# Key weights transposed on their way in, by two DMA queues, in a linear-attention and SiLU block

## The chip, the cores and the metric

The kernel runs on one core of a Trainium2 chip. A core has TensorE (PE, which does the matmuls and loads their weights), VectorE (DVE), ScalarE (ACT), GpSimd (POOL), SyncE (SP), and 16 DMA engines that carry what SP and ACT issue. The metric is the device time of one execution in microseconds (us); the median over runs is compared.

## The reference, cut to what matters

```python
h  = x + attention(layernorm(x))          # x: 2048 rows of 640, bf16
h2 = h + silu(layernorm(h) @ w1) @ w2     # w1: 640 x 1728, w2: 1728 x 640

# attention: 32 heads of width 20
q, k, v = split(xn @ wqkv)
pq, pk  = q @ w_phi[h], k @ w_phi[h]                     # per head, 20 x 20
phi_q   = [softmax(pq), softmax(-pq)]                    # over the 20 features
phi_k   = [softmax(pk), softmax(-pk)]
kv      = sum over rows of phi_k^T v;   z = sum over rows of phi_k
o       = (phi_q @ kv) / (phi_q . z);   result = o @ wo
```

## The kernel before

The 2048 rows are 16 tiles of 128 rows (`t` = 0 to 15); the 640 columns are 5 chunks of 128 (`c`). Each small operation is a Python function `op_xx`, and the string `ORDER` (lines 25 to 62) is a list of words such as `kp.3` (call `op_kp(3)`). Within one engine, and within each DMA queue, instructions run in the order of the words that concern it; the block `tc.manual_schedule` (line 678) fixes these orders, and the framework adds the semaphore waits that the data needs. A letter at a word's end names an engine or a queue: `.s` issues a DMA on SP, `.a` on ACT (or copies on ACT), `.v` works on DVE, `.p` on POOL. An instruction that waits holds back all that comes after it on its engine, DMA issues included.

Stages, and the words that the text uses:

- Head. `lx` loads tiles of x, `lp` loads `w_phi`, `lk` loads the key weights (tile `wk`), `lv` the value weights. `ph` (L189) spreads `w_phi` into a block form, `phb`, which uses the mask from `mk`. Key weights and `w_phi` are folded into one matrix, `Wfk`: `wt.c` transposes chunk `c` of `wk` on PE (five 128x128 transposes, L296), `wc.c` copies the result out of PSUM into `wTk`, `fk.c` multiplies with `phb` (six matmuls, L311), `fc.c` copies the result into `Wfk`. The query weights are folded in the same way (`gk`, `gc`, also L311), but they are read transposed: `lq.c` (L234) is a transposing DMA from DRAM, issued on SP into the tile `wTq`, which is the tile `wk` again, so that `lq.c` waits for `wt`.
- Layernorm of x: `st.t` (DVE statistics, L254 and L255), `rs` (POOL), `xn.t` (normalise, on DVE L271 or ACT L276), and a transpose of the tile, either on PE with a copy (`xt`, `xc`) or by a transposing DMA on SP (`xd`, L289).
- Keys and values, per tile: `kp` and `vp` (ten matmuls of 320 columns each, L339), `ke` (two exponentials, ACT, L361), `kr` (sums and reciprocals, DVE, L369 and L372), `ka` (product, POOL, L377; `kb` does half a tile on DVE), `vc` (copy of the values), `cc` (twenty small matmuls which add the tile to `kv`, L399). `km` (L409) masks the finished `kv`.
- Queries, in groups of four tiles: `qp.g.i` (matmuls of 512 columns, L419) and `qe` (exponentials, L429).
- From `dp.0` on (L453), which needs the finished `kv`: attention output per tile, normalisation, transposing DMA `td` (L508), projection `op` (L515), second layernorm, transposing DMA `hd` (L574), then `up` (L589), SiLU `ua` (L611), `yp` (L635) and the stores. This stage's orders are new too, its operations are the same. `ta` is a small exponential on ACT (L244), which makes ACT load the table of Exp at that point.

The warm-up: six matmuls of 512 columns on a zero tile ahead of the first word, with `ident` as the stationary operand, and `wm.256` or `wm.512` among the words (L248). Each `wm` among the words takes a PSUM buffer of its own. The pool `mm` has four such buffers, and every `wt`, `fk`, `gk`, `xt`, `kp`, `vp` and `wm` takes the next in turn, which waits until the user of that buffer four steps before has been copied out.

Of the kernel before, what the change touches and what calls it, by code (L numbers as in the profile page):

```python
# [34 lines left out]
xd.15 gk.0 kr.5 vp.9 ka.1.p gc.0.a xn.7.a kp.9 ke.8 xd.7 xn.12.v kr.0 ka.5.p kp.6 vc.9.a xd.11
xn.10.a kp.15 ke.6 xd.12 ka.0.p xd.13 cc.2 kr.6 cc.1 ke.15 cc.5 xd.10 vp.15 ke.9 kr.3 ka.6.p kp.11
vc.15.a xn.14.a kr.4 gk.1 vp.7 gc.1.a ka.3.p xd.14 ke.11 vp.11 lo.s l2.8.13.s vc.7.a kr.11 l1.0.s
ka.4.p vp.6 vc.11.a kp.13 kr.15 vc.6.a ka.11.p kp.12 kr.9 cc.4 ka.15.h cc.3 ke.12 cc.6 kr.8 cc.0
ka.9.p cc.11 ke.13 kp.14 kr.12 gk.3 ke.14 kp.10 ka.8.p gc.3.v kp.7 ke.10 kr.14 ka.12.p qp.1.2 ke.7
vp.14 kr.13 qe.1.2 qp.0.1 vc.14.a kr.7 ka.13.p vp.12 qe.0.1 ka.14.p vp.13 vc.12.v vp.10 vc.13.v  # L40
ka.7.p kr.10 qp.0.0 vc.10.a kb.15 ka.10.p qp.0.2 cc.13 qe.0.2 cc.15 cc.14 qe.0.0 cc.9 cc.7 cc.12
cc.10 cc.8 qp.2.2 km.1 close km.0 dp.0 qe.2.2 qp.1.1 dw.0.v dp.2 qe.1.1 dr.0 qp.1.0 dw.2.v do.0.0.p
do.0.1.p dp.3 qe.1.0 dr.2 qp.3.0 dw.3.v do.2.0.p dp.6 qe.3.0 dr.3 qp.2.0 dw.6.v do.3.0.p do.3.1.p
do.2.1.p td.3 dp.4 qe.2.0 dr.6 qp.3.1 dw.4.v td.0 do.6.0.p td.2 dp.1 qe.3.1 dr.4 qp.2.1 dw.1.v
do.4.0.p do.4.1.p do.6.1.p td.4 dp.5 qe.2.1 dr.1 op.0 dw.5.v do.1.0.p do.1.1.p qp.3.2 td.1 oa.0 dp.8
l1.2.s qe.3.2 dr.5 op.3 l2.4.8.s dw.8.v do.5.1.p sq.0 sa.0 op.1 sr.0 td.6 oa.3 do.5.0.p op.2 dr.8
td.5 oa.1 do.8.0.p dp.9 hn.0 do.8.1.p sq.1 op.4 dw.9.v sa.1 td.8 sr.1 op.6 hd.0 hn.1 oa.2 hd.1 op.5
oa.4 sa.2 sq.2 op.8 oa.6 sq.4 oa.5 sq.6 dp.7 sa.5 up.0.1 dw.7.v sa.6 sr.6 sr.2 up.0.2 oa.8 ua.0.1
dr.9 sa.8 sq.8 hn.6 do.9.0.v sr.8 do.9.1.v up.0.3 ua.0.2 dr.7 td.9 do.7.1.p dp.10 sq.5 up.0.0
do.7.0.p dw.10.v td.7 hd.6 op.9 hn.2 ua.0.0 hn.8 ua.0.3 hd.8 dp.12 sq.3 oa.9 op.7 sa.9 sq.9 yp.0.1  # L50
sr.9 oa.7 dw.12.v sq.7 sa.7 yp.0.0 sr.7 sa.4 hn.7 sa.3 yh.0.0 dr.10 hd.7 dp.11 hn.9 sr.4 yp.1.0
dw.11.v hd.9 do.10.1.p sr.3 yp.1.1 hd.2 do.10.0.v yo.0 dr.12 dp.14 hn.3 do.12.0.p up.2.2 dr.11
dw.14.v sr.5 do.11.0.p up.2.5 do.11.1.p ua.2.2 hn.4 dr.14 hd.4 hn.5 yo.1 do.12.1.v up.2.6 hd.3
ua.2.5 td.10 dp.15 up.2.4 dw.15.v td.12 td.11 op.10 do.14.1.v hd.5 dr.15 up.2.3 oa.10 sa.10 op.11
ua.2.3 sq.10 up.1.4 oa.11 ua.2.6 do.15.1.v sa.11 ta do.15.0.p up.1.1 do.14.0.p td.14 sq.11 up.2.1
td.15 ua.1.4 ua.1.1 up.1.3 ua.2.1 ua.2.4 up.1.6 ua.1.3 dp.13 ua.1.6 op.15 op.12 oa.15 dw.13.v sa.15
op.14 sr.10 up.1.5 sr.11 dr.13 hn.11 oa.14 up.2.0 do.13.1.v sa.14 sq.14 oa.12 ua.1.5 sa.12 do.13.0.p
up.1.2 ua.2.0 td.13 so.1 up.1.0 ua.1.2 sq.15 sr.15 op.13 ua.1.0 hn.15 sq.12 yp.5.1 oa.13 sa.13 sq.13
sr.14 yp.5.0 sr.12 yh.1.1 sr.13 yh.2.0 yo.5 yp.8.0 hn.10 hn.13 hd.13 yp.3.0 yp.6.0 hn.14 yp.8.1
yp.4.0 yo.8 so.8 hd.10 yp.6.1 so.0 yp.3.1 hn.12 hd.12 yp.4.1 yo.3 yo.6 so.3 hd.11 yp.2.0 hd.15  # L60
yp.9.0 hd.14 so.5 yh.1.0 yh.2.1 yp.9.1 yp.7.1 yo.9 yo.4 yp.7.0 so.4 so.9 so.6 up.4.0 yo.7 so.7
up.3.1 yp.2.1 ua.3.1 up.4.1 yo.2 ua.4.0 up.4.3 up.3.0 up.3.5 ua.3.0 ua.4.3 ua.4.1 up.3.3 up.3.4
ua.3.3 ua.3.5 up.4.2 up.3.6 ua.4.2 ua.3.4 up.3.2 ua.3.6 yp.15.0 ua.3.2 yp.10.0 yp.14.1 yh.3.0 yh.4.0
yp.12.1 yp.14.0 yp.12.0 yo.14 yp.15.1 yo.12 so.12 yp.11.1 yo.15 yp.11.0 so.15 so.14 so.2 yp.10.1
yh.3.1 yo.10 yq.13.0 yo.11 so.11 so.10 yq.13.1 yz.13.0 yz.13.1 sz.13.0.a sz.13.1.s
"""

@with_exitstack
def kernel(
# [41 lines left out]
    def mm2():  # L111
        return mm.tile([P, 2, 512], F32, name="mm2")
# [11 lines left out]
    wTk = first.tile([P, C, D], BF16, name="wTk")  # L124
# [3 lines left out]
    ident = persist.tile([P, P], BF16, name="ident")  # L128
    make_identity(nc, ident[:])
    warm = first.tile([P, 512], BF16, name="warm")  # L130
# [87 lines left out]
    def dma(q, out_, in_):  # L218
        (nc.sync if q == "s" else nc.scalar).dma_start(out_, in_)
# [13 lines left out]
    def op_lq(c):  # L233
        nc.sync.dma_start_transpose(wTq[:, :, c * P : (c + 1) * P], A_wqkv[c * P : (c + 1) * P, 0:D])  # L234

    def op_lo(q="s"):
        dma(q, wo[:], A_wo.rearrange("(c p) n -> p c n", p=P))

# [6 lines left out]

    def op_wm(n=512, ps=None):
        ps = mm2() if ps is None else ps
        nc.tensor.matmul(ps[:, 0, 0:n], ident[:], warm[:, 0:n], start=True, stop=True)  # L248
        return ps

    def op_st(t):
# [425 lines left out]
    ops = {k[3:]: f for k, f in locals().items() if k.startswith("op_")}  # L677
    with tc.manual_schedule(engines={PE, SP, POOL, DVE, ACT}):
        ps = None
        for i in range(6):  # L680
            ps = op_wm(512, ps)
        for word in ORDER.split():
            name, *args = word.split(".")
            ops[name](*[int(a) if a.isdigit() else a for a in args])
# [27 lines left out]
```

## Time and profile before

| | us |
|---|---|
| median of three runs | 243.97 (243.68 to 245.48) |
| the profiled execution's own time | 245.96 |
| span of the profiled execution, first to last instruction | 244.2 |
| PE busy | 234.6 |
| first warm-up matmul | 1.52 |
| first projection (`vp.1`) | 12.52 |
| first matmul of `dp.0` | 74.23 |
| last instruction on PE ends | 240.46 |

Times in the views count from the span's start. A timeline row gives start, length, engine, line of the kernel, the operation with what it writes and reads, and how many instructions were merged in the row. SPq and ACTq are the issuing side of the two DMA queues; an issue is not the transfer, whose time to landing stands in the DMA view. Busy PE is not PE at its peak, since matmuls overlap: the pitch of a row (its length over its count) tells more than the mean of one.

### The profile page before, as it was taken

How to read it: one execution, taken by the hardware profiler on the slowest of the kernel's cores; microseconds unless marked ns; L12 is line 12 of the kernel's file. 1: busy time of each engine (PE TensorE's matmuls, PEld its weight loads, DVE VectorE, ACT ScalarE, POOL GpSimd, SP SyncE). 2: the span in 40 equal slices, each digit the busy share in tenths (PEclk: the TensorE clock that was granted, in tenths of full speed). 3: DMA queues.
4: the chain of work that ended last, by engine and by line, in shares of the span. 5: the costliest groups of instructions: out<-in, count | busy, mean ns of one | idle time of the engine just before them, and what ended most of it. 6: DMA issues, size and time to landing. Idle time of an engine off the chain costs nothing.

```text
span 244.2 us, 5190 instructions
## 1 busy us (share of the span) xinstructions
PE 234.6 (96%) x2146; PEld 151.9 (62%) x2160; DVE 131.6 (54%) x252; ACT 108.1 (44%) x158; POOL 90.7 (37%) x172
## 2 busy tenths in 40 slices
PE   6999999998999999899899999999999999999995
PEld 3777677775674456577564545646776765556762
DVE  3599996899627999986597620722222310000223
ACT  3678988857444675266403098074000022450000
POOL 4244897997941446543473030325000000000000
PEclk9999999999999999999999999999999999999999
DMA  6899858580000046933442511020136300000022
GB/s 201 290 261 240 179 88 129 129 301 0 3 3 3 0 82 143 253 26 66 44 82 56 108 29 27 1 54 4 27 82 136 107 30 0 0 3 0 10 100 81
DMA packets 42968, 20.60 MB, mean 84 GB/s; under 512 B 34368, under 2 KB 42560, under 8 KB 42944
## 3 DMA queue, kind: packets, MB, share of 16 engines
q1 hardware_dynamic: 42368, 19.65, 34.9%
q10 hardware_dynamic: 576, 0.62, 0.7%
q8 instruction: 17, 0.28, 0.5%
q14 instruction: 7, 0.06, 0.1%
HBM read 9.61 MB, written 2.62 MB: 50 GB/s over the span
## 4 chain that ended last, share of the span: by engine, by line
PE 76%; DMA 9%; DVE 7%; ACT 3%; issue 2%; POOL 1%; ACTq 0%; SPq 0%; POOLq 0%
PE mm L635 23%; PE mm L589 21%; PE mm L419 9%; PE mm L339 8%; PE mm L515 6%; DVE Sk L369 3%; PE mm L453 2%; DMA X<-in_A_x_dram 2%; DMA wk<-in_A_wqkv_dram 2%; DMA ot<-o 2%; DMA XnT<-xn 2%; DMA HnT<-hn 2%; PE mm L399 2%; ACT Ek L361 1%; PE mm L650 1%
## 5 line engine op out<-in xcount | busy, mean ns | idle before, releaser
L589 PE MATMUL mm<-HnT,w 128*128 128x512 bf16 (+1 forms) x318 | 57.8, 336 | 0.6 <-DMA HnT<-hn 0.2
L635 PE MATMUL mm<-w,shT 128*128 128x320 bf16 (+2 forms) x415 | 57.8, 299 | 0.2 <-issue 0.2
L611 ACT ACTIVATE shT<-mm 128x1024 bf16<-128x1024 f32 (+2 forms) x29 | 27.0, 963 | 65.7 <-PE mm L589 64.2
L635 PEld LDWEIGHTS <-shT 128*128 128x128 bf16 x416 | 39.8, 98 | 17.5 <-issue 1.1
L589 PEld LDWEIGHTS <-w 128*128 128x128 bf16 x325 | 31.3, 98 | 23.7 <-issue 0.5
L658 DVE TENSOR_TENSOR ob<-mm,X 128x640 bf16<-128x640 f32 x15 | 12.2, 822 | 53.7 <-PE mm L635 44.7
L339 PEld LDWEIGHTS <-XnT 128*128 128x128 bf16 x320 | 30.8, 98 | 13.4 <-issue 0.8
L377 POOL TENSOR_TENSOR Ek<-Ek,Sk 128x1280 bf16<-128x1280 bf16 (+1 forms) x16 | 36.6, 2321 | 3.6 <-DVE Sk L372 2.3
L429 ACT ACTIVATE EqT<-mm 128x1024 bf16<-128x1024 f32 (+1 forms) x24 | 19.8, 881 | 12.8 <-PE mm L419 12.8
L515 PE MATMUL mm<-wo,ot 128*128 128x320 bf16 x160 | 23.4, 299 | 1.8 <-DMA ot<-o 1.8
L339 PE MATMUL mm<-Wfk,XnT 128*128 128x320 bf16 x160 | 23.5, 299 | 1.2 <-DVE Wfq L159 0.6
L369 DVE TENSOR_REDUCE Sk<-Ek 128x64 f32<-128x1280 bf16 x16 | 23.2, 1448 | 2.4 <-ACT Ek L361 2.4
L488 POOL TENSOR_TENSOR o<-u,rd 128x320 bf16<-128x320 f32 x25 | 18.0, 736 | 16.8 <-DVE rd L482 7.5
L419 PE MATMUL mm<-XnT,Wfq 128*128 128x512 bf16 x94 | 23.1, 380 | 0.4
L339 PE MATMUL mm<-wv,XnT 128*128 128x320 bf16 x160 | 23.2, 299 | 0.0
L361 ACT ACTIVATE Ek<-mm 128x640 bf16<-128x640 f32 x32 | 20.5, 708 | 5.7 <-PE mm L399 3.2
L524 DVE SCALAR_TENSOR_TENSOR X<-mm,X 128x640 bf16<-128x640 f32 x16 | 12.9, 818 | 17.4 <-PE mm L515 17.3
L515 PEld LDWEIGHTS <-ot 128*128 128x128 bf16 x160 | 15.2, 98 | 8.6 <-DMA ot<-o 2.3
L532 ACT ACTIVATE sq<-X 128x640 bf16<-128x640 bf16 x16 | 11.7, 734 | 15.5 <-DVE X L524 15.5
L537 POOL TENSOR_SCALAR HM<-HST 128x1 f32<-128x1 f32 x16 | 3.4, 213 | 34.3 <-DVE X L524 34.3
L419 PEld LDWEIGHTS <-Wfq 128*128 128x128 bf16 x100 | 9.2, 97 | 10.2 <-issue 0.3
L254 DVE BATCH_NORM_STATS2 stats<-X 128x6 f32<-128x320 bf16 x32 | 13.7, 469 | 2.9 <-DMA X<-in_A_x_dram 2.9
(73 smaller groups left out, 209.9 us busy)
## 6 DMA issues: line engine op xcount, KB each, us to landing
out_dram<-ob SPq DMA_DIRECT2D x15, 160.0 KB, 1.9
w<-in_B_w_dram SPq DMA_DIRECT2D x3, 720.0 KB, 5.0
X<-in_A_x_dram SPq DMA_DIRECT2D x3, 640.0 KB, 5.5
w<-in_B_w_dram SPq DMA_DIRECT2D x2, 640.0 KB, 6.3
wo<-in_A_wo_dram SPq DMA_DIRECT2D x1, 800.0 KB, 5.0
w<-in_B_w_dram SPq DMA_DIRECT2D x1, 800.0 KB, 6.6
X<-in_A_x_dram SPq DMA_DIRECT2D x4, 160.0 KB, 4.4
wv<-in_A_wqkv_dram SPq DMA_DIRECT2D x2, 320.0 KB, 4.8
```

What stands on the lines that cost most here:

```text
L254: nc.vector.bn_stats(stats[:, k, :], X[:, t, k * 320 : (k + 1) * 320])
L339: nc.tensor.matmul(ps[:, half, 0:320], tok(XnT[t // GT], t)[:, c, :], W[:, c, half * 320 : (half + 1) * 320], start=(c == 0), stop=(c == C ...
L361: nc.scalar.activation(Ek[:, s, :].rearrange("p (a n) -> p a n", a=2), tl["kp", t][:, :, 0:320], AF.Exp, scale=1.0 - 2.0 * s,)
L369: nc.vector.tensor_reduce(Sk[:], tl["ek", t][:].rearrange("p s (h f) -> p (s h) f", f=DH), axis=AX.X, op=ALU.add,)
L377: eng.tensor_tensor(Ek3, Ek3, tl["sk", t][:, lo:hi].unsqueeze(2).to_broadcast([P, hi - lo, DH]), op=ALU.mult,)
L419: nc.tensor.matmul(ps[:, k, :], Wfq[:, c, r * P : (r + 1) * P], XnT[g][:, c, :], start=(c == 0), stop=(c == C - 1),)
L429: nc.scalar.activation(E[:, s, rs[0] : rs[-1] + 1, :], tl["qp", g, i][:, 0 : len(rs), :], AF.Exp, scale=1.0 - 2.0 * s,)
L488: (nc.vector if eng == "v" else nc.gpsimd).tensor_tensor(tl["o", t][:, a * 320 : (a + 1) * 320].rearrange("p (h f) -> p h f", f=DH), tl["u ...
L515: nc.tensor.matmul(ps[:, half, 0:320], tl["ot", t][:, c, :], wo[:, c, half * 320 : (half + 1) * 320], start=(c == 0), stop=(c == C - 1),)
L589: nc.tensor.matmul(ps[:, i * W : (i + 1) * W], w1[:, c, fc * P : (fc + 1) * P], HnT[g][:, c, 0:W], start=(c == 0), stop=(c == C - 1), skip ...
L611: nc.scalar.activation(sh[:, a:b], tl["up", g, k][:, 0 : b - a], AF.Silu)
L635: nc.tensor.matmul(ps, shT[g][:, fc * W + i * P : fc * W + (i + 1) * P], w2[:, fc, a:b], start=first and fc == 0, stop=last and fc == FC - ...
```

## The change

`wTk` is no longer made on PE. A new word, `lt.c`, reads chunk `c` of the key weights transposed from DRAM straight into `wTk`, on SP (`.s`) or ACT (`.a`): three on SP, two on ACT. The words `lk`, `wt` and `wc` are gone, and `lq` no longer shares its tile with a loaded `wk`. The warm-up takes a part of the zero tile as the stationary operand instead of `ident`, has eight matmuls instead of six, and ten `wm` among the words instead of six (five of them of 512 columns). `ORDER` is another list for all engines: in the head tiles 3, 2 and 0 come first instead of 1 and 0, all five folds of the key weights stand before the first projection, the loads of x and of the value weights are spread over both queues, and 30 query matmuls stand ahead of `dp.0` instead of 35. `ta` moves from among the SiLU calls to a place among the last exponentials of the keys. The diff, with the list cut to the part up to the second half of the key stage:

```diff
 ORDER = """
-lk.4.5.a lx.1.2.s lk.2.3.a lp.s lk.0.1.a lk.3.4.s mk lx.0.1.s lk.1.2.s lv.4.5.s lv.0.2.s st.1
-lv.2.4.s wt.2 lx.2.3.s wt.4 wc.2.a ph rs.1 lx.3.4.s wm.256 wm.256 wt.0 lx.4.8.s wc.4.a xn.1.v wc.0.a
-wm.256 wm.256 fk.4 st.0 wt.3 fc.4.a fk.2 wt.1 wc.3.a xt.1 rs.0 wc.1.v lq.4 fc.2.a wm.256 fk.3 fk.1
-xn.0.v fc.3.a fk.0 xc.1.v lx.8.12.s fc.0.a lx.12.16.s wm.256 xt.0 vp.1 lq.3 st.2 xc.0.a fc.1.a st.3
-vp.0 lq.2 st.4 rs.3 l2.0.4.s kp.0 vc.0.a lh.s rs.2 xn.3.v vc.1.a st.5 gk.4 ke.0 xt.3 xn.2.v kp.1
-rs.4.2 st.8 xc.3.a xn.4.v xt.2 ke.1 st.9 vp.3 xd.4 xn.5.v gc.4.a st.11 kp.3 xd.5 xc.2.a st.10 kp.2
-l1.1.s ke.3 st.13 rs.8.4 vp.2 ke.2 st.6 rm.8 rm.9 st.14 mo gk.2 vc.3.a kp.5 xn.8.a st.15 rm.10
-gc.2.a mc xd.8 kp.4 st.12 vc.2.a xn.9.a st.7 lq.1 vp.4 ke.5 rs.12.4 kr.2 lq.0 vp.5 ke.4 rm.11 rm.14
-xd.9 rs.6.2 vc.4.a xn.13.v vp.8 xn.15.v xn.11.a rm.7 xn.6.v ka.2.p kr.1 xd.6 vc.5.a kp.8 vc.8.a
-xd.15 gk.0 kr.5 vp.9 ka.1.p gc.0.a xn.7.a kp.9 ke.8 xd.7 xn.12.v kr.0 ka.5.p kp.6 vc.9.a xd.11
-xn.10.a kp.15 ke.6 xd.12 ka.0.p xd.13 cc.2 kr.6 cc.1 ke.15 cc.5 xd.10 vp.15 ke.9 kr.3 ka.6.p kp.11
-vc.15.a xn.14.a kr.4 gk.1 vp.7 gc.1.a ka.3.p xd.14 ke.11 vp.11 lo.s l2.8.13.s vc.7.a kr.11 l1.0.s
...
+lp.a lx.3.4.s lx.2.3.a lt.3.s lt.4.a mk lt.1.s mc lx.0.1.a lx.1.2.a lt.2.s lt.0.a ph st.3 lq.0
+lx.4.8.a wm.512 wm.512 fk.4 lv.0.2.a st.2 wm.512 wm.256 fk.1 rs.3 fc.4.a lv.2.4.s fk.3 fc.1.a
+lx.8.12.s xn.3.v wm.512 wm.256 fk.2 rs.2 lq.3 fc.3.a st.0 wm.256 xt.3 fk.0 fc.2.a xn.2.v fc.0.a lq.1
+rs.0 wm.512 wm.256 gk.0 xc.3.v xt.2 lv.4.5.a wm.256 kp.3 xn.0.v xc.2.a lq.4 gc.0.a st.4 xt.0
+lx.12.16.a kp.2 lq.2 xc.0.a st.5 st.1 kp.0 rs.4.2 ke.2 rs.1 xn.4.v vp.0 ke.3 st.6 xd.4 mo xn.1.v
+ke.0 vp.3 st.7 lh.s vc.0.a st.11 rs.6.2 gk.2 gk.4 gc.2.a kp.4 xn.5.v rm.6 st.10 gc.4.a xd.5 vc.3.a
+gk.3 xn.7.v gk.1 st.8 xd.7 vp.4 gc.1.a gc.3.a st.9 l1.1.s xt.1 vc.4.a vp.2 l1.2.s st.14 rs.8.4
+xc.1.a ke.4 st.13 kp.5 rm.11 rm.10 st.15 vc.2.a kp.1 xn.6.a st.12 xn.11.a kp.7 xn.9.v rs.12.4 ke.1
+kr.4 xd.9 vp.7 ke.5 rm.8 rm.12 lo.s rm.13 kr.0 ka.4.p xn.10.a qp.0.1 vc.7.a xd.10 ke.7 kr.2 ka.0.p
+vp.9 xd.11 xn.13.a qe.0.1 kr.3 vp.5 xd.13 ka.2.p xd.6 kp.9 vc.9.a kr.5 xn.12.a l2.4.8.s vp.1 ke.9
+ka.3.p xd.12 xn.15.v kp.11 kr.1 vc.5.a l2.8.13.s ka.5.p cc.2 cc.4 xn.14.v ke.11 cc.0 kr.9 xd.14 cc.3
+kp.13 vc.1.a ka.1.p l1.0.s xn.8.a kr.11 kp.10 ke.13 xd.8 vp.6 ka.9.p ke.10 xd.15 vp.10 l2.0.4.s
+kr.10 kp.6 vc.10.a vc.6.a kr.13 ka.10.p kp.14 ke.6 kp.8 kr.7 ka.11.h cc.5 ka.13.p cc.9 kr.6 ke.14
+cc.1 cc.10 vp.11 kr.14 ka.6.p vp.8 vc.11.a ke.8 qp.0.2 ka.14.p vc.8.a kr.8 vp.12 kp.12 vc.12.a kb.11
...
 """
         nc.sync.dma_start_transpose(wTq[:, :, c * P : (c + 1) * P], A_wqkv[c * P : (c + 1) * P, 0:D])
 
+    def op_lt(c, q="s"):
+        (nc.sync if q == "s" else nc.scalar).dma_start_transpose(
+            wTk[:, :, c * P : (c + 1) * P], A_wqkv[c * P : (c + 1) * P, D : 2 * D],
+        )
+
     def op_lo(q="s"):
         dma(q, wo[:], A_wo.rearrange("(c p) n -> p c n", p=P))
 
@@ -245,7 +250,7 @@
 
     def op_wm(n=512, ps=None):
         ps = mm2() if ps is None else ps
-        nc.tensor.matmul(ps[:, 0, 0:n], ident[:], warm[:, 0:n], start=True, stop=True)
+        nc.tensor.matmul(ps[:, 0, 0:n], warm[:, 0:P], warm[:, 0:n], start=True, stop=True)
         return ps
 
     def op_st(t):
@@ -677,7 +682,7 @@
     ops = {k[3:]: f for k, f in locals().items() if k.startswith("op_")}
     with tc.manual_schedule(engines={PE, SP, POOL, DVE, ACT}):
         ps = None
-        for i in range(6):
+        for i in range(8):
             ps = op_wm(512, ps)
         for word in ORDER.split():
             name, *args = word.split(".")
```

## The prediction

> **What bounds the kernel now.** I read the page's busy parts first, then the timeline of the head, then who keeps PE waiting, then the DMA views.
>
> ```profile
> PE 234.6 (96%) x2146; PEld 151.9 (62%) x2160; DVE 131.6 (54%) x252; ACT 108.1 (44%) x158; POOL 90.7 (37%) x172
> PE   6999999998999999899899999999999999999995
> ```
>
> PE bounds nearly the whole span. A change can win only in the head (first two digits), in PE's few waits, and in the tail.
>
> Timeline, PE (start, length, line; a bracket holds the idle time before):
>
> ```profile
> 1.52 2.74 PE L248 MATMUL mm<-warm,ident 128*128 128x512 bf16 x6 [1.52 <-POOL ident masks.py:199]
> 8.02 0.76 PE L311 MATMUL mm<-phb,wTk 128*128 128x140 bf16 x6
> 12.52 2.88 PE L339 MATMUL mm<-wv,XnT 128*128 128x320 bf16 x20
> 24.26 0.48 PE L311 MATMUL mm<-phb,wk 128*128 128x140 bf16 x6
> 74.23 0.57 PE L453 MATMUL mm<-KVBD,EqT 64*128 64x88 bf16 x20
> ```
>
> Dense projections start at 12.52 and run into `dp.0` at 74.23. The same fold costs 0.76 us at 8.02 and 0.48 at 24.26: PE is slow until about 10.7, though the granted clock reads 1.00 throughout.
>
> Who kept PE waiting (us in total, times, longest):
>
> ```profile
> PE mm L515 <- DMA ot<-o: 1.8, 2, 1.2
> PE mm L248 <- POOL ident masks.py:199: 1.5, 1, 1.5
> PE mm L296 <- DMA wk<-in_A_wqkv_dram: 0.7, 2, 0.4
> PE mm L339 <- DVE Wfq L159: 0.6, 1, 0.6
> PE mm L339 <- DMA XnT<-xn: 0.5, 1, 0.5
> PE mm L589 <- DMA HnT<-hn: 0.2, 1, 0.2
> PE mm L635 <- issue: 0.2, 1, 0.2
> ```
>
> All but the second and third lie behind 12.52: 3.3 us is the most that new orders can win there.
>
> Timeline, ACT's and SP's queues, and the ScalarE table load:
>
> ```profile
> 0.79 1.46 ACTq L219 DMA_DIRECT2D wk<-in_A_wqkv_dram  x3
> 0.79 0.40 SPq L219 DMA_DIRECT2D X<-in_A_x_dram  x1
> 2.28 1.28 ACT L161 ACT_TABLE_LOAD   x1 [2.28 <-issue]
> 10.47 1.29 SPq L234 DMA_TRANSPOSE wk<-in_A_wqkv_dram  x1
> ```
>
> An issue holds its queue 0.46 us for a plain load, 1.3 for a transpose. The table load stands behind all of ACT's first issues.
>
> DMA view of the stretch around 10.5, then the queues of the whole run:
>
> ```profile
> wk<-in_A_wqkv_dram SPq DMA_TRANSPOSE x1, 2.9
> ```
> ```profile
> q1 hardware_dynamic: 42368, 19.65, 34.9%
> q10 hardware_dynamic: 576, 0.62, 0.7%
> ```
>
> From issue to landing a 160 KB transpose takes 2.9 us on a quiet queue (median of the five 4.2, longest 7.4). ACT's queue, q10, carries 576 packets of about 1 KB, plain loads and one store: before never transposes on two queues.
>
> **The change part by part.** The sum goes against the profiled execution: span 244.2, its run 245.96. The median of the three runs is 243.97; I carry the change of span over to it.
>
> Removed: five `wk` loads, 25 PE transposes (`wt`, about 0.53 us per five) and five copies (`wc`, 0.5 to 0.7 each), all ahead of 12.52. Nothing later needs them.
>
> Added: five transposed loads, in the order `lt.3.s lt.4.a lt.1.s lt.2.s lt.0.a lq.0` over both queues. The framework sets this program's waits; the orders do not. How it treats transposes from two queues no row shows. From below it costs nothing (both queues run abreast; a gain over that has no source). From above, a transpose of one queue is held until those of the other have landed: four hand-overs of a landing each, 2.9 to 7.4 us. I take the upper kind: I read the framework, which orders by semaphores whatever it counts as sharing a path, as letting the transposes of only one queue run at a time. And I take 2.9 for each, because the first X load at 0.79, also on quiet queues, lands after 3.1.
>
> The Trainium skill, "DMA: Bandwidth & Descriptors", section "DMA Transpose (X-bar)", speaks for this: two streams of transposes in flight corrupt each other, so the later must wait for the earlier's full completion. By that rule the hand-over is needed; without it the sum would be that of rival 1 below. No run here shows it.
>
> The walk: SP issues X at 0.79 and `lt.3` at 1.25, landing 4.15. ACT, held there, issues `lt.4`, landing 7.05. SP, held, issues `lt.1` at 7.15 and `lt.2` at 8.5, landing 11.4. ACT issues `lt.0` at 11.45, landing 14.35. Behind the waits stand, on SP, `lq.0 lv.2.4 lx.8.12` and the other `lq` (from 14.4); on ACT, `lx.0.1 lx.1.2` (5.5) and, after `lt.0` (12.75), `lx.4.8 lv.0.2` (2 x 0.46), the table load (1.28), and so `fc.4` at 15.0. That is the costly part: ACT's five weight copies stand in its program behind the last transpose.
>
> From 15.0 PE and ACT alternate, because four PSUM buffers are shared by folds and warm-ups: `fk.3` waits for `fc.4`'s buffer, `fk.2` for `fc.1`'s, `gk.0` for `fc.0`'s. At warm prices (fold 0.35 to 0.48, copy 0.70, transposes 0.28) the first projection `kp.3` starts at 19.4; at the cold ones of 8.02 to 10.9 (fold 0.76, transposes 0.58) at 20.7. PE sits nearly idle from 9 to 15, so most is cold: 20.3.
>
> One sentence stands apart: the Trainium skill, "TensorE: Matmul & The Clock Gate", Part 1, has the clock fall to half after an idle window of about 3.4 us, which agrees with the 0.76 against 0.48; warm all along it would be 19.4.
>
> Warm-up: eight 512-column matmuls at 0.43 (2.74 over six, less one latency) and two more, from 1.25 instead of 1.52, as they need only DVE's memset. They end by 5.6; nothing waits for PE before 7.05. Fillers between folds lie beside ACT's copies. Both cost nothing; were the copies faster, each filler would cost 0.11 to 0.43 us.
>
> `ta` moves into the Exp stage: two table loads of 1.28 go where ACT waits 64.2 us for PE in all. Nothing.
>
> From `kp.3` to `dp.0`: 32 projections x 1.36 = 43.5; four Wq folds x 0.35 = 1.4; two tile transposes, 0.5; sixteen `cc` x 0.43 = 6.9; 30 query matmuls x 0.216 = 6.5 (before did 35 there). Sum 58.9, so 79.2. From `dp.0` to PE's end before: 240.46 - 74.23 = 166.2, less its waits of 2.2, plus the five query matmuls 1.1: 165.1. Tail unchanged: 244.2 - 240.46 = 3.7. Waits under the new order: between 0 and the present 3.3, middle 1.7.
>
> Is PE still the last at `dp.0`? DVE stands still at `xc.3` until 19.1; then 13 statistics x 1.0, six `xn` x 0.4 and the first Sk, 2.0, give 36.5. POOL's sixteen products (36.6 busy, 3.6 waiting in before) end at 76.7, one `cc` and one mask later 77.8: 1.4 ahead of PE. Late X tiles are what comes next: `lx.4.8` now issues at 12.75, before by 7.4.
>
> Sum: 20.3 + 58.9 + 165.1 + 1.7 + 3.7 = 249.7, against 244.2: +5.5. On the median about 249.5; I say 249.8 for the extra hops of the four hand-overs.
>
> **The rivals.**
>
> 1. No hand-over: queues abreast (ends on the other side). ACT issues `lt.0` at 3.97, its last load by 6.2, table load to 7.5, and the same chain at warm prices puts `kp.3` at 11.9. Sum 11.9 + 58.9 + 165.1 + 1.7 + 3.7 = 241.3, -2.9: 241.1 on the median, 239.4 with no waits, 242.7 with 3.3. For it: no row shows a wait between queues, and the issue order alternates. Against it: all 49 transposes of before are issued by SP (q1) while q10 is nearly empty, so no row shows two queues transposing at once either, and my reading of the framework. It decides when one hand-over costs under about 1 us.
>
> 2. POOL or DVE sets `dp.0`. If `lx.4.8` or `lx.8.12` land as late as the 7.4 us that loads near 12.9 took, DVE's statistics start 1 to 2.5 us later and POOL passes PE: `dp.0` near 81.5, time 251.8. For it: the 1.4 us of slack. Against: the needed tiles come first in DVE's order.
>
> 3. The hand-overs come cheaper: landing 2.6 as the on-chip transposes, all warm, all waits closed: 249.5 - 1.2 - 0.9 - 1.6 = 245.8.
>
> **How the numbers follow.** Forecast 0.65; rival 1 0.14; rival 2 0.15; rival 3 0.06. Time 249.8. From the unknowns: low is rival 3, 246.0; high is rival 2 with landings of 3.5 instead of 2.9 (+2.2), 254.0. Rival 1 and the edges are left out, under 0.2. One per cent of 243.97, about what a measurement here can tell, puts the bounds at 241.5 and 246.4. Rival 1 splits 0.08 faster, 0.06 same; of rival 3 0.02 is same; the rest is slower: 0.84.
>
> **What would show it.** Right: the `lt` issues as rows on both queues with starts near 1.3, 4.2, 7.2, 8.5 and 11.5, ACT's queue held; ACT's table load near 14; first L344 matmul near 20; `dp.0` near 80; PE waits on copies in the head. Wrong: all five issues done by 5.3 and projections before 12.5 (rival 1); POOL's last product later than PE's last projection (rival 2).

## The result and the profile after

The changed kernel is slower: median 255.59 us (253.92 to 258.51, four runs) against 244.12 us for the kernel before (243.68 to 245.48, four runs), a ratio of 1.0438 with a 95% interval of 1.0377 to 1.05. The profiled execution took 256.59 us, its span is 254.9. The ratio leaves out the slowest run of the changed kernel, so it gives a loss of 10.7 us where the medians give 11.5. The prediction was 249.8 us, with a range of 246 to 254: right in sign and in the main mechanism, too small by half.

The page of the changed kernel: PE's busy time, PE's row and the granted clock in 40 slices of 6.4 us, and the chain that ended last by engine.

```profile
PE 235.3 (92%) x2123; PEld 151.2 (59%) x2141; DVE 134.9 (53%) x251; ACT 103.9 (41%) x155; POOL 89.9 (35%) x169
...
PE   6329799999999999999999999999999997999995
...
PEclk9657999999999999999999999999999999999999
...
PE 78%; DMA 16%; SPq 3%; DVE 1%; issue 1%; ACT 1%; ACTq 0%; DVEq 0%
```

PE's busy sum hardly moved (234.6 before). The loss is idle time: the second, third and fifth slices read 3, 2 and 7 where before has 9 in each, and the granted clock falls in the second to fourth. From the sixth slice on the row is nearly as full as before. In the chain that ended last, DMA now holds 16% (9% before).

The chain of waits of the changed kernel in the first 32 us (start, length, what):

```profile
1.26 3.69 DMA wTk<-in_A_wqkv_dram
4.97 2.90 DMA wTk<-in_A_wqkv_dram
7.88 1.20 SPq L237
...
9.13 1.28 SPq L237
...
10.45 3.09 DMA wk<-in_A_wqkv_dram
13.56 4.07 DMA wTk<-in_A_wqkv_dram
17.64 1.20 SPq L234
...
21.52 9.74 DMA wk<-in_A_wqkv_dram
```

Read it as a baton: each transposing load starts where the one of the other queue has landed. SP's `lt.3` lands at 4.95, ACT issues `lt.4` at 4.97; that lands at 7.87, SP issues `lt.1` at 7.88. The last row is a query block that takes 9.74 us from issue to landing.

PE's timeline in the changed kernel, the rows that answer to 8.02, 12.52, 24.26 and 74.23 of before, and ACT's table load:

```profile
7.92 0.49 PE L316 MATMUL mm<-phb,wTk 128*128 128x140 bf16 x6 [2.26 <-DMA wTk<-in_A_wqkv_dram]
11.51 1.38 PE L316 MATMUL mm<-phb,wTk 128*128 128x140 bf16 x12 [2.78 <-DMA wTk<-in_A_wqkv_dram]
18.10 0.37 PE L253 MATMUL mm<-warm 128*128 128x256 bf16 x1 [4.78 <-ACT Wfk L161]
18.26 0.80 PE L316 MATMUL mm<-phb,wTk 128*128 128x140 bf16 x6
22.20 1.70 PE L344 MATMUL mm<-Wfk,XnT 128*128 128x320 bf16 x10
31.31 0.80 PE L316 MATMUL mm<-phb,wk 128*128 128x140 bf16 x12 [1.71 <-DMA wk<-in_A_wqkv_dram]
83.67 0.56 PE L458 MATMUL mm<-KVBD,EqT 64*128 64x88 bf16 x20
```
```profile
16.06 1.28 ACT L161 ACT_TABLE_LOAD   x1 [16.06 <-DMA wv<-in_A_wqkv_dram]
17.36 2.48 ACT L161 CAST Wfk<-mm 128x640 bf16<-128x640 f32 x4
```

The first projection starts at 22.20 instead of 12.52, 9.7 us of the 10.7 by which the span grew. From there to `dp.0` it is 61.5 (61.7 before), from `dp.0` to the end 171.2 (170.0 before).

Who kept PE waiting in the changed kernel:

```profile
PE mm L316 <- DMA wTk<-in_A_wqkv_dram: 5.0, 2, 2.8
PE mm L253 <- ACT Wfk L161: 4.8, 1, 4.8
PE mm L316 <- DMA wk<-in_A_wqkv_dram: 1.7, 1, 1.7
PE mm L594 <- DVE ob L663: 1.4, 1, 1.4
...
```

Where before lost 0.7 us to key weights, 9.8 us now go to them and to the copies behind them.

One thing has to be put right in the description of the kernel before: the four PSUM buffers are not handed out strictly in turn. `fk.1` and `fk.3` ran in the row at 11.51, and `fk.3`, the fourth user behind `fk.4`, did not wait for the copy `fc.4` at 17.36. What waited for a buffer, 4.8 us, was the warm-up matmul behind them.

### The profile page after: what moved, and what is told of

Same layout as the page of the kernel before. It is cut to its first block, busy times and chain, and to the rows that moved or that the text cites. A ratio compares the mean times of both kernels' runs of the same rounds, so it can differ in the third digit from the quotient of the medians.

```text
span 254.9 us, 5146 instructions
## 1 busy us (share of the span) xinstructions
PE 235.3 (92%) x2123; PEld 151.2 (59%) x2141; DVE 134.9 (53%) x251; ACT 103.9 (41%) x155; POOL 89.9 (35%) x169
## 4 chain that ended last, share of the span: by engine, by line
PE 78%; DMA 16%; SPq 3%; DVE 1%; issue 1%; ACT 1%; ACTq 0%; DVEq 0%
PE mm L640 21%; PE mm L594 21%; PE mm L344 11%; PE mm L424 9%; PE mm L520 8%; DMA wk<-in_A_wqkv_dram 5%; DMA wTk<-in_A_wqkv_dram 4%; PE mm L458 3%; DMA XnT<-xn 3%; PE mm L404 2%; DMA out_dram<-ob 2%; SPq L234 1%; PE mm L604 1%; DMA ot<-o 1%; DMA HnT<-hn 1%; SPq L237 1%
## 5 line engine op out<-in xcount | busy, mean ns | idle before, releaser
L594 PE MATMUL mm<-HnT,w 128*128 128x512 bf16 (+1 forms) x316 | 58.5, 335 | 2.1 <-DVE ob L663 1.4
L640 PE MATMUL mm<-w,shT 128*128 128x320 bf16 (+2 forms) x415 | 58.7, 299 | 0.1
L616 ACT ACTIVATE shT<-mm 128x1024 bf16<-128x1024 f32 (+2 forms) x29 | 27.1, 963 | 63.9 <-PE mm L594 58.9
L344 PEld LDWEIGHTS <-XnT 128*128 128x128 bf16 x320 | 31.0, 98 | 13.1 <-DMA XnT<-xn 0.9
L493 POOL TENSOR_TENSOR o<-u,rd 128x320 bf16<-128x320 f32 x22 | 16.6, 766 | 38.3 <-DVE rd L487 31.0
L529 DVE SCALAR_TENSOR_TENSOR X<-mm,X 128x640 bf16<-128x640 f32 x16 | 12.9, 818 | 19.4 <-PE mm L520 19.2
L559 DVE TENSOR_SCALAR hn<-X,HM 128x640 bf16<-128x640 bf16 x16 | 7.1, 462 | 14.2 <-DMA HnT<-hn 7.2
```

The source lines that it names most:

```text
L344: nc.tensor.matmul(ps[:, half, 0:320], tok(XnT[t // GT], t)[:, c, :], W[:, c, half * 320 : (half + 1) * 320], start=(c == 0), stop=(c == C ...
L493: (nc.vector if eng == "v" else nc.gpsimd).tensor_tensor(tl["o", t][:, a * 320 : (a + 1) * 320].rearrange("p (h f) -> p h f", f=DH), tl["u ...
L594: nc.tensor.matmul(ps[:, i * W : (i + 1) * W], w1[:, c, fc * P : (fc + 1) * P], HnT[g][:, c, 0:W], start=(c == 0), stop=(c == C - 1), skip ...
L616: nc.scalar.activation(sh[:, a:b], tl["up", g, k][:, 0 : b - a], AF.Silu)
L640: nc.tensor.matmul(ps, shT[g][:, fc * W + i * P : fc * W + (i + 1) * P], w2[:, fc, a:b], start=first and fc == 0, stop=last and fc == FC - ...
```

## The experiments

The theory to test: the loss is made in the head, by the hand-overs between two transposing queues. Its rivals: the cold clock, the slowness of the transposed read itself, and the new orders. Ratios are to the kernel before, run on the same chip beside each.

**One queue alone.** All five loads on SP.

```diff
-... lt.3.s lt.4.a mk lt.1.s mc lx.0.1.a lx.1.2.a lt.2.s lt.0.a ph
+... lt.3.s lt.4.s mk lt.1.s mc lx.0.1.a lx.1.2.a lt.2.s lt.0.s ph
```

> The changed kernel with all five transposed key loads on SP, nothing else moved. Theory (the four hand-overs between the two transposing queues cost the time): the five issues stand back to back, 1.3 us apart, between 1.3 and 7.8; nobody waits on SP for a key chunk; the first key projection starts near 12 instead of 22.2, and the time is about 255.6 - 10 - 1 = 244.5 (243 to 246). Rival A (a transposed read from DRAM is slow in itself, on any queue): first projection after 17, time over 250. Rival B (the new orders cost it): first projection near 12, but the time stays over 248.

Measured: 250.09 us (247.67 to 251.72), ratio 1.0203 [1.012, 1.0287], so 5.5 us less than the changed kernel (5.7 by the ratios). SP's issues, and PE's head:

```profile
1.26 8.52 SPq L237 DMA_TRANSPOSE wTk<-in_A_wqkv_dram  x5
9.82 1.28 SPq L234 DMA_TRANSPOSE wk<-in_A_wqkv_dram  x1
```
```profile
8.48 0.78 PE L316 MATMUL mm<-phb,wTk 128*128 128x140 bf16 x6 [3.06 <-DVE stats L259]
13.77 0.80 PE L316 MATMUL mm<-phb,wTk 128*128 128x140 bf16 x6
15.83 1.52 PE L344 MATMUL mm<-Wfk,XnT 128*128 128x320 bf16 x10
```

All five are issued by 9.78 (14.8 in the changed kernel) with no wait for another queue, and the first projection comes 6.4 us earlier. The row at 8.48 names DVE, but `phb` had been done since 4.74; PE's weight load at 8.47 waited for the key block. The hand-overs are shown, at about half the loss. The rest is not they, and the theory's 243 to 246 was missed: the first projection at 15.83 lies between the cases, and the folds still cost 0.6 to 0.8 us each. The profiled execution took 247.67 us, 2.4 below the median, so its rows show this head at its best.

**One hand-over.** Two loads first on ACT, then three on SP.

```diff
-lp.a lx.3.4.s lx.2.3.a lt.3.s lt.4.a mk lt.1.s mc lx.0.1.a lx.1.2.a lt.2.s lt.0.a ph
+lt.4.a lt.0.a lx.3.4.s lx.2.3.s lp.s lx.0.1.s lt.3.s mk lt.1.s mc lx.1.2.a lt.2.s ph
```

> The changed kernel with one hand-over left: two key loads first of all on ACT, then three on SP and the query loads behind them; the X tiles 3, 2 and 0 and the small weights go to SP. Theory: SP's first transposed load starts when ACT's second has landed, near 5 to 6, first projection near 14 to 15, so some 2.5 to 3 us later than with all on SP: about 247 (245.5 to 249). Rival A: over 250, like the changed kernel. Rival B: over 248, and not tied to the first projection.

Measured: 250.61 us (249.81 to 251.21), ratio 1.0253 [1.0183, 1.0322]; first projection at 17.27. SP's row and PE's largest wait:

```profile
7.07 3.93 SPq L237 DMA_TRANSPOSE wTk<-in_A_wqkv_dram  x3
```
```profile
PE mm L316 <- DMA wTk<-in_A_wqkv_dram: 4.4, 1, 4.4
```

ACT had issued both of its loads by 3.43 and SP its last plain load by 2.92; SP then stood until 7.07, a single hand-over of about 4 us. The first projection is 1.4 us later than with one queue, but the two times cannot be told apart (ratios 1.0253 and 1.0203). The theory's 245.5 to 249 was missed and the time is over the 250 of rival A: the wait is shown, its price in the time is not.

**The warm-up filled** with matmuls on the zero tile, in the changed kernel: 8 instead of one `wm` ahead of `fk.4`, 13 ahead of `fk.1`, 22 behind `fk.3` (`wf.n` is n matmuls in one PSUM buffer).

```diff
-... wm.512 wm.512 fk.4 ... wm.512 wm.256 fk.1 ... xn.3.v wm.512 wm.256 fk.2 ...
+... wm.512 wf.8 fk.4 ... wm.512 wf.13 fk.1 ... xn.3.v wf.22 wm.256 fk.2 ...
```

> The changed kernel, both queues kept, with PE's three idle stretches of the head (5.6 to 7.9, 8.7 to 11.5, 13.3 to 17.6) filled with more zero matmuls, so that the clock should not fall. Theory (the hand-overs set when the data are there, and a cold clock makes the folds behind them slow as well): folds 0.35 to 0.48 instead of 0.6 to 0.8, first projection about 1.5 us earlier than 22.2, all else unchanged, so the profiled span near 253 instead of 254.9. Rival (the clock does not matter here, since ACT's copies set the pace): first projection within 0.3 us of 22.2.

Measured: 257.45 us (256.45 to 258.57), ratio 1.0559 [1.0518, 1.06]: a miss. The rows show why:

```profile
18.18 0.59 PE L252 MATMUL mm<-warm 128*128 128x512 bf16 x1 [6.11 <-ACT Wfk L160]
18.99 6.71 PE L252 MATMUL mm<-warm 128*128 128x512 bf16 x21 [0.22 <-issue]
27.68 1.52 PE L348 MATMUL mm<-Wfk,XnT 128*128 128x320 bf16 x10
```

The last fillers needed a PSUM buffer that only ACT's copy freed, so they did not fill the gap but ran behind it, 6.7 us on the path. The folds behind them are warm (0.48), yet the first projection comes 5.5 us later; `dp.0` is 3.3 us later (86.94), and the median 1.9. So the trial says nothing against the clock, only that a filler placed behind a wait delays what follows.

**One queue, warm.** The kernel with all loads on SP, with 14 fillers ahead of the first fold and 4 ahead of the second, where nothing is waited for.

```diff
-lx.4.8.a wm.512 wm.512 fk.4 lv.0.2.a st.2 wm.512 wm.256 fk.1
+lx.4.8.a wm.512 wf.14 fk.4 lv.0.2.a st.2 wm.512 wf.4 fk.1
```

> The one-queue version with the idle stretch before its first fold (5.4 to 8.5) filled with zero matmuls. Clock theory: folds at 0.35 to 0.48, first projection about 1.5 to 2 us earlier than the 15.8 there, span near 244, time 1 to 2 us lower and less spread from run to run. Data theory (late landings and ACT's late table load set the head): first projection within 0.7 us of 15.8.

Measured: 246.89 us (245.77 to 248.53), ratio 1.0109 [1.0069, 1.0149], 3.2 us less than without the fillers. PE:

```profile
1.24 7.76 PE L252 MATMUL mm<-warm 128*128 128x512 bf16 x23 [1.24 <-DVE warm L130]
8.84 0.48 PE L320 MATMUL mm<-phb,wTk 128*128 128x140 bf16 x6
14.11 1.52 PE L348 MATMUL mm<-Wfk,XnT 128*128 128x320 bf16 x10
23.35 1.14 PE L320 MATMUL mm<-phb,wk 128*128 128x140 bf16 x12 [2.01 <-DMA wk<-in_A_wqkv_dram]
```

The fold at 8.84 costs 0.48 where it cost 0.78, and the first projection is 1.7 us earlier, 0.3 of it because a key block landed sooner. The granted clock, as a mean over the execution, is 0.985 to 0.986 in the four runs without these fillers and 0.993 to 1.0 in the four with them. The cold clock is shown as the second part of the loss; its size is less sure, since the intervals of the two ratios overlap (by the ratios it is 2.3 us). The spans of the two profiled executions do not show it (246.7 with the fillers, 245.8 without): this one took 248.53 us, 1.6 over its median, the other 2.4 below. About 1.1% remains, with a wait of 2.0 us for a query block in sight.

**Are the transposed reads starved by plain loads?** One queue; the table load early, and ACT's 640 KB load of x and the value weights later.

```diff
-... lx.0.1.a lx.1.2.a lt.2.s lt.0.s ph st.3 lq.0 lx.4.8.a wm.512 wm.512 fk.4 lv.0.2.a ...
+... lx.0.1.a lx.1.2.a ta lt.2.s lt.0.s ph st.3 lq.0 wm.512 wm.512 fk.4 ... fc.1.a lx.4.8.a ... fc.3.a lv.0.2.a ...
```

> The one-queue version with ACT's queue freed: the 640 KB load of X tiles 4 to 7 and the value weights' first load go behind ACT's second and third weight copy, and a small exponential at the start makes ACT load its table there. Data theory: transposed loads land after about 3 us instead of 6.6, as no large plain load runs beside them; first fold near 6, copies from about 6.3 instead of 10.2, first projection at 11 to 12.5, time 243 to 246. Clock theory: no change of the clock's own, so the first projection stays after 14.

Measured: 254.31 us (250.63 to 254.64), ratio 1.0347 [1.0258, 1.0436]: a miss. First the windows of this kernel, then of the kernel before with the new warm-up (below), each from 4 to 8 us; the last two numbers are the busy share of the DMA engines and GB/s.

```profile
4.00:8.00 4.00, 1.69 (x4) 0.30 (x2) 3.89 (x10) 0.32 (x2) 2.61 (x6) 1.00 1.15 179
```
```profile
4.00:8.00 4.00, 2.98 (x33) 1.75 (x32) 3.18 (x7) 2.06 (x4) 1.56 (x2) 1.00 1.05 342
```

With transposed reads the DMA engines are as busy and move about half as much. The key blocks landed after a median of 4.8 us instead of 5.9, not 3, and the first projection came at 15.04, 0.8 us earlier. What was pushed back then came late elsewhere: PE waited 3.3 us for a query block and 1.5 for value weights.

**The transposed read in the old orders.** The kernel before, with the five loads transposed on SP and `wt` and `wc` gone.

```diff
-lk.4.5.a lx.1.2.s lk.2.3.a lp.s lk.0.1.a lk.3.4.s mk lx.0.1.s lk.1.2.s ... wt.2 ... wc.2.a ...
+lt.4.s lx.1.2.s lt.2.s lp.s lt.0.s lt.3.s mk lx.0.1.s lt.1.s ...
```

> The kernel before, its orders kept, with the five key loads made transposing loads on SP, and the PE transposes and their copies left out. Theory: no hand-over, the head loses five groups of PE transposes and five copies; first projection at 10.5 to 12 instead of 12.5; time 242 to 244.5. Rival A: first projection after 15, time over 246. Rival B says nothing here: orders are the old ones, so it expects 244 or less.

Measured: 249.82 us (249.24 to 251.17), ratio 1.0233 [1.017, 1.0296]; first projection at 15.47. PE's first two waits:

```profile
PE mm L315 <- DVE phb L188: 3.2, 1, 3.2
PE mm L315 <- DVE XnT L158: 2.1, 1, 2.1
```

By its numbers this is rival A's case (over 246, first projection after 15), but the five reads landed in 2.9 to 3.8 us, so slow landings are not its reason. One queue of transposes costs the old orders as much as the new (1.0203), by another way: each issue holds SP 1.2 to 1.3 us, so `w_phi` goes out at 4.04 (1.25 before), and `phb` and the first tile come late.

**The new orders with the old read.** Plain loads, and the PE transposition and its copy put straight ahead of each fold.

```diff
-... lt.3.s lt.4.a ... fk.4 ... fk.1 ...
+... lk.3.4.s lk.4.5.a ... wt.4 wc.4.a fk.4 ... wt.1 wc.1.v fk.1 ...
```

> New orders and new warm-up, but the key weights read plainly and transposed on PE with copies by ACT and DVE, as before the change; the query weights go to a tile of their own (rows of w2 that are loaded later). Theory (hand-overs alone): no hand-over, first projection near 13 to 14, time 245 to 247. Rival A (transposed read slow): clearly faster than the version with all transposed loads on SP. Rival B (new orders): over 248.

Measured: 251.47 us (248.61 to 254.31), ratio 1.0254 [1.0165, 1.0342]. Inconclusive: transposition, copy and fold in a row made PE wait 4.7 us for copies, and the granted clock fell to 0.50, with the first projection at 21.43, in the profiled execution (254.31 us, 2.8 over the median). This says nothing of the orders.

**The warm-up part alone**, in the kernel before: zero tile as the stationary operand, eight matmuls.

```diff
-        nc.tensor.matmul(ps[:, 0, 0:n], ident[:], warm[:, 0:n], start=True, stop=True)
+        nc.tensor.matmul(ps[:, 0, 0:n], warm[:, 0:P], warm[:, 0:n], start=True, stop=True)
...
-        for i in range(6):
+        for i in range(8):
```

> The kernel before with the warm-up part of the change alone: eight matmuls instead of six, zero tile as the stationary operand. Both theories: no difference that can be told (within 0.5 per cent of before), first projection between 12.0 and 12.7.

Measured: 243.5 us (242.81 to 243.96, ten runs), ratio 0.999 [0.9968, 1.0011]: nothing, as the prediction's term had it. In its profiled execution the first projection is at 11.11 and the span 241.7; the profiled execution of before, with folds of 0.76 us and 12.52, took 245.96 us, 1.8 over the median. The loss of the changed kernel is therefore better read from the medians.

**No transposed key read at all, all else as changed.** The kernel leaves the transposition out.

```diff
-        (nc.sync if q == "s" else nc.scalar).dma_start_transpose(
-            wTk[:, :, c * P : (c + 1) * P], A_wqkv[c * P : (c + 1) * P, D : 2 * D],
+        dma(
+            q, wTk[:, :, c * P : (c + 1) * P],
+            A_wqkv[c * P : (c + 1) * P, D : 2 * D].rearrange("p (r k) -> p r k", r=C),
```

> The changed kernel, with its five key-weight loads on the same two queues at the same places, but as plain 160 KB loads of the same blocks: the values are not transposed, so the output is not the reference's, and that alone is changed in what is computed. Theory (the loss lies in the transposed reading: hand-overs, the cold clock behind them, its slow landing): no load waits for another, the folds run with the data, the first L344 projection at 11.5 or sooner (22.2 in the changed kernel), and the time is 241 to 244. Rival (the new orders of the engines cost by themselves, whatever the reading): the time stays above 246 with the first projection before 13.

Measured: 247.51 us (246.22 to 247.91), ratio 1.0108 [1.0056, 1.016]: 8.1 us of the 11.5 gone, but a miss for the theory, since 1.1% is left with no key block transposed on its way: the rival's case, but for a first projection at 13.25 instead of before 13. As much is left with all five transposed on one queue and PE kept warm, though the first projection is 0.9 us later there (14.11). PE:

```profile
6.87 0.49 PE L317 MATMUL mm<-phb,wTk 128*128 128x140 bf16 x6 [1.41 <-DMA wTk<-in_A_wqkv_dram]
12.53 0.49 PE L317 MATMUL mm<-phb,wk 128*128 128x140 bf16 x6 [0.54 <-DMA wk<-in_A_wqkv_dram]
13.25 1.52 PE L345 MATMUL mm<-Wfk,XnT 128*128 128x320 bf16 x10
21.59 0.81 PE L317 MATMUL mm<-phb,wk 128*128 128x140 bf16 x12 [1.11 <-DMA wk<-in_A_wqkv_dram]
```

The rows point at what the new orders ask for: the first query fold (on `wk`, at 12.53) stands ahead of the first projection, where before had it at 16.59, behind three, and the next two stand some 8 us later. Query blocks are transposed on their way in both kernels. The run also bounds rival A: all that the transposed read of the key weights costs, hand-overs, slower landing and the cold clock that follows from PE's waits, is these 8.1 us. With one queue 2 to 3 us of them are left, and a warm PE takes these away too, so a price of the slower landing by itself does not show in the time.

**PE transposes placed as the data come**, with the new orders from `gk.0` on and plain key loads in the order of before.

```diff
-lp.a lx.3.4.s lx.2.3.a lt.3.s lt.4.a mk lt.1.s mc lx.0.1.a lx.1.2.a lt.2.s lt.0.a ph st.3 lq.0 ...
+lk.4.5.a lx.3.4.s lk.2.3.a lp.s lk.0.1.a lk.3.4.s mk lx.2.3.s mc lk.1.2.s lv.0.2.s lx.0.1.s lx.1.2.s
+wt.4 wt.2 wc.4.a ph wm.256 wt.0 wc.2.a st.3 fk.4 rs.3 wt.3 wc.0.v fc.4.a lx.4.8.s lv.2.4.s fk.2 wt.1 ...
```

> The changed kernel's orders from the first projection on, but its key weights read plainly and transposed on PE, with the loads on SP and ACT and the transposes placed as the data arrive, the zero-tile warm-up kept. Theory (the orders behind the head are neutral, the loss is the transposed reading): the first projection at 11 to 13, then 230 to 232 to the end, a time of 242 to 245, level with the kernel before. Rival (orders of the changed kernel cost or gain by themselves): over 246, or under 241, with the first projection in the same place.

Measured: 248.07 us (247.1 to 248.29), ratio 1.0134 [1.009, 1.0178]: a miss for both. All folds of the key weights were done by 10.2, and then:

```profile
14.17 0.78 PE L316 MATMUL mm<-phb,w 128*128 128x140 bf16 x6 [3.91 <-DMA w<-in_A_wqkv_dram]
```

PE stood 3.9 us for the first query block (here in a tile `w`) and came back cold; the first projection starts at 15.28.

**The query products later** in that kernel, all five behind the ninth projection.

```diff
-... wm.256 gk.0 xt.2 kp.3 ... gk.2 gk.4 gc.2.a kp.4 ... gk.3 xn.7.v gk.1 st.8 xd.7 vp.4 ...
+... wm.256 xt.2 kp.3 ... kp.4 ... xn.7.v st.8 xd.7 vp.4 gk.0 gc.0.a gk.2 gk.4 gc.2.a gc.4.a gk.3 gk.1 ...
```

> The kernel with the new orders, plain key loads and PE transposes (248.07 us, where PE waited 3.9 us for the transposed read of the first query block, whose product the new orders put ahead of the first projection), with the five query products gk and their copies moved behind the ninth projection, nothing else. Theory (the new orders' one cost of their own is that they ask for the transposed query blocks too early): the 3.9 us wait goes, the first projection at 10.5 to 11.5, 230 to 232 from it to the end, 242.5 to 245. Rival (the query reads only mask another lateness of the new orders): another wait takes its place and the time stays over 246.5.

Measured: 248.8 us (248.0 to 250.76), ratio 1.021 [1.0167, 1.0252]. The rival's case. The wait for the query block is gone, and this is next:

```profile
12.37 0.45 PE L287 MATMUL mm<-ident,xn 128*128 128x128 bf16 x5 [2.33 <-DVE xn L276]
12.65 1.52 PE L344 MATMUL mm<-Wfk,XnT 128*128 128x320 bf16 x10
```

`xt.2` stands ahead of the first projection and waits for the second tile's layernorm; with five query products in a row, PE then waits 1.7 us for ACT's copies.

**The same move in the one-queue, warm kernel**, with the same edit.

> The kernel with all key reads transposed on SP and the warm-up filled (246.89 us; first projection at 14.11, then a wait of 2.0 us for a query block), with the five query products gk and their copies moved behind the ninth projection. Theory (what is left over the kernel before is the transposed key reads, about 1 us late, and the query blocks asked for too early): the 2.0 us wait and the fold ahead of the first projection go, first projection at 13.4 to 13.8, 243.5 to 245, so level with before or up to 0.5 per cent slower. Rival (slow transposed reads hold something else, the value weights or X tiles): another DMA wait of 1.5 us or more shows and the time stays over 246.

Measured: 251.15 us (249.84 to 258.09), ratio 1.0254 [1.0206, 1.0302]: again the rival's case. First projection at 14.25, then

```profile
PE mm L349 <- DMA XnT<-xn: 3.4, 2, 3.0
...
PE mm L349 <- DMA wv<-in_A_wqkv_dram: 1.0, 1, 1.0
```

**The early query product put alone into the kernel before.**

```diff
-... wm.256 xt.0 vp.1 lq.3 ... vc.1.a st.5 gk.4 ke.0 ...
+... wm.256 xt.0 gk.4 vp.1 lq.3 ... vc.1.a st.5 ke.0 ...
```

> The kernel before, with one PE step moved: the first query product (gk.4), which stood three projections in, put ahead of the first projection, as the new orders have it; nothing else. Theory (part of what the new orders lose in the head is that they ask for a transposed query block too early): its read is issued at 8.8 to 10.5 and lands 4 to 5 us later, so PE waits 2 to 4 us ahead of the first projection, first projection at 13.5 to 15, the time 1 to 4 us over before, 245 to 248. Rival (the early query product is hidden anyway): same as before within 0.4 per cent.

Measured: 246.06 us (245.43 to 248.11, nine runs), ratio 1.0093 [1.0061, 1.0126], 2.0 us over before, the theory's case at the low end, with a shorter wait (1.6 us) than the 2 to 4 expected:

```profile
13.15 0.49 PE L311 MATMUL mm<-phb,wk 128*128 128x140 bf16 x6 [1.61 <-DMA wk<-in_A_wqkv_dram]
13.48 2.88 PE L339 MATMUL mm<-wv,XnT 128*128 128x320 bf16 x20
```

**The early demands taken out of the new orders**, in the kernel with PE transposes: two projections of one tile ahead of the next tile's transposition, the first query product behind the third projection, value weights loaded sooner.

```diff
-... wm.256 gk.0 xt.2 kp.3 xn.0.v xc.2.a lq.3 lq.1 gc.0.a st.4 xt.0 kp.2 xc.0.a st.5 st.1 kp.0 ...
+... wm.256 kp.3 lq.3 lq.1 vp.3 xt.2 xn.0.v xc.2.a vc.3.a xt.0 kp.2 xc.0.a gk.0 ke.3 st.4 gc.0.a kp.0 ...
```

> The kernel with the new orders, plain key loads and PE transposes, with the value weights loaded right behind the key weights, the first two projections (key and value of the same tile) put ahead of the next tile's transposition, and the first query product behind the third projection. Theory (behind the head the new orders are worth the same as the old, so removing the head's early demands is enough to reach the kernel before): first projection at 10 to 11, no wait over 1 us up to 30 us, 242 to 245. Rival (the new orders cost by themselves further on): 246 or more with no wait in the head.

Measured: 245.78 us (244.93 to 246.34, twelve runs), ratio 1.0073 [1.0047, 1.0099]: the best of the kernels with the new orders, and outside the expectation, since before is still 1.7 us better. The first projection begins at 10.06, the earliest of all, but PE runs into its own inputs. Its waits from there to 45 us:

```profile
PE mm L344 <- DMA XnT<-xn: 1.3, 2, 0.8
PE mm L287 <- DVE xn L276: 0.8, 1, 0.8
PE mm L344 <- ACT Wfk L161: 0.8, 1, 0.8
```

Against the kernel before with the new warm-up, in the profiled executions (spans 244.3 and 241.7), the first projection is 1.1 us earlier, but the stretch from there to `dp.0` is 3.0 us longer (64.0 against 61.0), with 3.9 us of named waits in it against 0.6, and the rest is 0.6 us longer.

No version with the new orders or a transposed key read beat the kernel before.

## Why the prediction was wrong in size

The span came to 254.9 us against a sum of 249.7. Of the 5.2 us between them 1.9 lie ahead of the first projection (22.20 against 20.3), 2.8 in PE's waits behind it (4.5 against 1.7) and 0.5 in the work (228.2 against 227.7, the sum's 58.9, 165.1 and 3.7).

**Right: the hand-over.** The forecast had `lt.4` held until `lt.3` lands and `lt.1` until `lt.4` lands. The chain shows it (4.95 to 4.97, 7.87 to 7.88), and with one queue it is gone. The Trainium skill, "DMA: Bandwidth & Descriptors", section "DMA Transpose (X-bar)", asks for just that wait between two streams; by that rule the hand-over follows, and the trace agrees; it cost 5.5 us of median. Rival 1 fell with it.

**Wrong step 1: the walk to ACT's copies** (table load "near 14", measured 16.06). `fc.4` came 2.4 us later than forecast (17.36 against 15.0), mostly by two terms. The landing was taken as 2.9 us for each; measured 3.7 for `lt.3`, 2.9 for `lt.4`, 3.7 for `lt.2`, 4.1 for `lt.0`. And the forecast let ACT's `lt.0` go straight after SP's `lt.2`; SP's query load `lq.0`, also a transpose, went out first at 10.45, and `lt.0` waited for its landing until 13.56, about 0.7 us. The baton goes in the order in which the program issues the transposes, which need not be that of the words: `lt.0` stands ahead of `lq.0` in `ORDER`.

**Wrong step 2: the buffers.** The forecast let folds and warm-ups take PSUM buffers strictly in turn, so that `fk.3` would wait for `fc.4`. Only a warm-up did. So two folds were done sooner than forecast, which gave back some 0.5 us of step 1: the first projection came at 22.20, predicted 20.3.

**Rivals 2 and 3 fell too.** POOL's last product of the key stage ended at 80.35, 3.3 us ahead of `dp.0`, and PE's waits name POOL nowhere. No landing of a key block came down to the 2.6 us of rival 3.

**The clock, right in kind, too small.** The windows of the changed kernel show the granted clock, third number from the right, while PE waits:

```profile
8.00:10.00 2.00, 0.73 (x8) 0.34 (x8) 0.87 (x2) 0.00 (x0) 0.00 (x0) 0.72 0.79 211
10.00:22.20 12.20, 5.91 (x47) 4.89 (x48) 2.85 (x10) 4.46 (x6) 0.87 (x2) 0.50 0.84 236
```

0.50 for 12 us. The forecast gave the cold clock 0.9 us of walk (20.3 against 19.4); in the one-queue kernel, keeping PE warm brought 1.7 us in the head and 2 to 3 in the time. The Trainium skill, "TensorE: Matmul & The Clock Gate", Part 1, has the clock at half after an idle window of about 3.4 us. The trace agrees on the half but not on the length: the granted clock reads 1.00 up to 8.75 and 0.50 from 9.0, and the longest idle stretch of PE before that was 2.3 us, so the measurement decides.

**Wrong step 3: "between 0 and the present 3.3, middle 1.7"** for the waits behind the first projection. They came to 4.5 us, 1.7 of it for a query block that landed 9.74 us after its issue. The trace of before had shown no transposed read over 7.4. It was also the wrong kind of bound: new orders can make new waits.

**Right: the work behind the head.** From the first projection to the last instruction, less PE's named waits in it, before takes 231.7 - 3.3 = 228.4 us and the changed kernel 232.7 - 4.5 = 228.2; the other profiled kernels lie between 227.5 and 230.0. The changed kernel's time is thus set by when the projections start and by what they then wait for. The spread of 2.5 us among kernels is as large as the part of the loss that stays open below, so this sum alone does not clear the later orders.

**Wrong by omission: the price of the head's orders.** The forecast priced the new order of PE's steps only where the transposed key read delayed it. By the medians, the 11.5 us divide as follows: 5.5 hand-overs (changed kernel to one queue), 3.2 cold clock (one queue to warm), 2.8 that remain; by the ratios 5.7, 2.3 and 2.7. The middle part is the least sure: the two ratios' intervals overlap (1.012 to 1.0287, 1.0069 to 1.0149), and the head's timeline gives 1.7 us for it. The plain loads leave 1.1% too, so the new orders lose that much without any transposed key read; that it is the same loss in the warm one-queue kernel is inferred. That an early query product alone costs 0.9% is shown in the kernel before. Whether it is the whole of the rest is open: each time one early demand was taken out, another wait took its place (layernorm of the second tile, its transposition by DMA, value weights), and the best rearrangement kept 0.7%. In its profiled execution that rest lies behind the first projection, mostly in named waits up to `dp.0`; which order carries it was not separated.

**Why no part gains.** The removed 25 transposes and five copies cost no time: PE waits in the head in any case, and with the PE transposes in place the folds were done by 10.2 us, sooner than with any transposed read (13.1 in the warm one-queue kernel).

## What to carry to other kernels

Before a transposing load is put on a second queue, write down the order in which the program issues all transposes, and add a landing for each change of queue: here four changes cost 5.5 us. One queue has no such waits, but each of its issues holds it 1.3 us, and with all five on it both orders were still 2% slower than before. Operations removed from an engine are worth nothing in a stretch where that engine waits; price such a change by when the first dense stage can start, and then list every input that the new order asks for before it. If a stall of several microseconds ahead of PE is unavoidable, fill it with matmuls that depend on nothing, and place them where no buffer is waited for: such fillers won 2 to 3 us where PE was waiting for data, and lost 1.9 us of median behind a wait for a buffer.

## What the runs showed of the hardware

- A 160 KB transposed read from DRAM took 2.9 to 4.1 us from issue to landing in the changed kernel's key blocks, a median of 5.9 in the one-queue kernel beside plain 640 KB loads, and 9.74 for a query block of the changed kernel. With such reads in flight the DMA engines were as busy as with plain ones (1.15 against 1.05) at half the throughput (179 against 342 GB/s). The Trainium skill, "Advanced Engine Details and Errata", section "X-Bar Transpose (TRN2)", has transposing DMAs as fast as plain ones; in these windows they are not, and the measurement decides.
- The granted clock read 1.00 throughout the first 16 us of before although its folds took 0.76 us at 8.02 instead of 0.48, and throughout the first 24 us of the one-queue kernel with the late loads, whose folds took 0.70 to 0.80 up to 12.58. So the length of equal rows is the safer sign in a head.
- The granted clock fell to 0.50 after PE had stood idle for 2.3 us and then 0.8 us of work (changed kernel, near 8.9), and stayed there until after 22.
